# Fewer bytes in the SBUF copies, five of sixteen issued by GpSimd, tau on GpSimd's queue, and a new table of priorities

## The chip, the cores and the metric

The kernel runs on one core of a Trainium2 chip. The time is device microseconds of one execution; the figure that counts is the median of several runs of the same program. An engine is TensorE (PE, with PEld for its weight loads), VectorE (DVE), ScalarE (ACT), GpSimd (POOL) or SyncE (SP, which here only issues DMAs).

## What is computed

Attention over 4 batches x 8 heads, 576 positions, head width 64, with a threshold below the row's maximum; then two feed-forward layers over 2304 tokens, model width 512, inner width 2048, all in float32:

```python
scores = scale * np.matmul(q, k.transpose(0, 1, 3, 2))
thresh = np.max(scores, axis=-1, keepdims=True) - tau
scores = np.where(scores >= thresh, scores, -1000000000.0)
attn = np.exp(scores - np.max(scores, axis=-1, keepdims=True))
attn = attn / (np.sum(attn, axis=-1, keepdims=True) + 1e-09)
attn_out = np.matmul(attn, v)                                   # heads are put side by side: x, 2304 x 512
h = x @ w_in;   x = np.where(h > 0.0, h, np.exp(np.minimum(h, 0.0)) - 1.0) @ w_out
h = x @ w2_in;  x = np.maximum(0.01 * h, h) @ w2_out
```

## The kernel before

**Stages.** Attention is cut into 32 groups: a pair of heads (16 of them) times a half of the query rows, in units of 64 rows; a group has 4 or 5 units. Beside attention, TensorE runs the first half (inner slices f = 0 to 7) of the first feed-forward layer over seven blocks of 256 tokens, as the attention output of those tokens comes free. When attention ends its memory is closed, and the rest follows: one block of 512 tokens with f = 0 to 7, then all tokens in blocks of 512 with f = 8 to 15, then the second layer with f = 0 to 15.

**A unit.** `qk` (L458) writes the scores of a unit to PSUM tile `s`, out of the loaded tile `in`. VectorE scales them and finds the row's maximum (L462, into `ss`) and makes the threshold (`thr`, L468). ScalarE applies the threshold (L473) and the exponential (L476, into `e`). VectorE takes the reciprocal of the sum (`su`, L479), GpSimd multiplies `e` by it (L481).

**Turning.** The matmul with v (L564) needs `e` with keys on the partitions. In the first four groups TensorE transposes it (L496). In the other 28, VectorE transposes 32x32 blocks into a tile `t` (L501), and sixteen DMAs inside SBUF, 32 partitions each, bring the blocks of `t` into their places in a tile `p` (L550): copy (a, d) goes from quadrant a of `t` to quadrant d of `p`. Each row of such a copy holds five column blocks c = 0 to 4. A score row has 576 keys, which is 4.5 times 128, so of the fifth block the partitions 64 to 127 (quadrants d = 2 and 3) are zeros. Of the sixteen copies SyncE issues 13 and GpSimd 3. The matmul runs `v` a group later (`held`).

**Feed-forward beside and after it.** `step_h` (L603 in full float32 for the first block, L606 in three passes for the others) fills PSUM tile `h`; ScalarE takes its exponential (L621), VectorE or GpSimd subtract one (L623, L625), VectorE merges with `h` (L629, into `g`, in the first block into `gh`), ScalarE rounds the result to `gh` (L311), and VectorE or GpSimd form the rest `gl` = g - gh (L305, L306). `step_y` (L656, L660) multiplies by the second weights two steps later.

**Weights** come as raw 64-bit words (`wraw`, L324) and are put together by GpSimd or ScalarE (L328, L336) and by VectorE in two steps (L341, L344); then `split_w` rounds them (`wih`, `woh`, L309 or L311) and takes the rest (`wil`, `wol`). For f = 8 to 15 and for the second layer all weights pass one after the other through a single buffer `w15`.

**Order.** Nothing is scheduled on the chip: `Order.run` lists every engine's instructions when the program is built. Each operation has a due time (`vt`) that is worked out from the table `KN`, and the operations that are ready are taken in that order with assumed costs; letters in `KN` say which engines may do an operation (`ko`: the rest of a weight outside the first eight slices; `kv`: the copy of the v matmul's result out of PSUM). On the chip each engine takes its list in order and waits where an operand isn't there.

Of the kernel before, what the change touches and what calls it, by code (L numbers as in the profile page):

```python
# [259 lines left out]
def attn_moe_kernel(ctx, tc, kqv, tau, w1i, w1o, w2i, w2o, yp, out):  # L260
# [21 lines left out]
    ysx = mp.tile([128, KC, TB], F32, name="ysx")  # L282
    ys_r = Ring(lambda: ysx, 1)
# [133 lines left out]
    ld = op(sp(128, 4, lambda: nc.sync.dma_start(out=taut, in_=tau.partition_broadcast(128))), [], [], KN["tl"])  # L417
    tau_op = op((DVE, 450, taus), [ld], [], -9e5)
# [3 lines left out]
    def group(gi, p, vts):  # L422
# [4 lines left out]
        kq, v = in_r.new(), v_r.new()  # L427
        cut = 2 * HALF + 128 * n
        ld = [op(sp(128, 4 * cut, lambda: nc.sync.dma_start(
            out=kq()[:, 0:cut], in_=kqv[gi * NE + p][:, 0:cut])), [], [kq], due)]  # L430
        lv = op(sp(128, 2560, lambda: nc.sync.dma_start(
            out=v().rearrange("p h c d -> p (h c d)"), in_=kqv[gi * NE + p][:, KQV - 10 * D:KQV])), [], [v], due + KN["vl"])

# [104 lines left out]
        return lambda: values(gi, p, n, w, vts[n - 1] + KN["o3"], by_pe, turned, tg, pg, v, lv, blocks)  # L538

    def values(gi, p, n, w, vt, by_pe, turned, tg, pg, v, lv, blocks):  # L540
        b, u0, u1 = GROUPS[gi]
        got = turned
        if not by_pe:
            got = []
            for z, (a, d) in enumerate((a, (a + r) % 4) for r in range(4) for a in range(4)):
                to = pg, slice(32 * d, 32 * d + 32), slice(5 * a * w, 5 * a * w + 5 * w)
                fr = tg, slice(32 * a, 32 * a + 32), slice(5 * d * w, 5 * d * w + 5 * w)
# [192 lines left out]
    for gi, (b, u0, u1) in enumerate(GROUPS):  # L740
        for p in range(NE):
            later = group(gi, p, [(u + j) * TU for j in range(u1 - u0)])
            u += u1 - u0
            if held is not None:
                held()
            held = later
            if gi < GP or p in PT or u == NP * NU:
                held()
                held = None
        ends.append((b * S + 64 * u1, u))  # L750
# [116 lines left out]
```

## Time and profile before

| | |
|---|---|
| median of 3 runs | 1052.46 us (1051.07 to 1056.69) |
| the profiled execution, its own time | 1050.85 us |
| its span, first to last instruction | 1049.1 us |
| busy PE / DVE / ACT / POOL | 1007.5 / 599.6 / 497.4 / 307.4 us |
| mean granted TensorE clock | 0.992 |

The profiled execution is 1.6 us below the median of the runs and lies within their range; 1.75 us of its time are outside the span. Attention ends at about 408 us of the span. Busy times overlap, so they don't add up to the span; the idle time of TensorE is what a change can win.

### The profile page before, as it was taken

What the parts mean: (1) busy time and instruction counts of PE and PEld (TensorE: products, weight loads), DVE (VectorE), ACT (ScalarE), POOL (GpSimd) and SP (SyncE); (2) the same over time, 40 slices, a digit from 0 to 9 for tenths busy, and PEclk for the clock granted to TensorE, in tenths of its full rate; (3) what the DMA queues carried; (4) which work ended last, traced back from release to release, by engine and by line L of the source; (5) the groups of instructions that cost most, each with busy time, mean ns of one, the idle gap of its engine ahead of it and who ended that gap; (6) DMA issues with size and microseconds to landing.
All of it is one profiled execution on the core that took longest, in us unless ns stands there. A gap on an engine that the chain in (4) does not pass through costs nothing.

```text
span 1049.1 us, 17092 instructions
## 1 busy us (share of the span) xinstructions
PE 1007.5 (96%) x6228; PEld 794.7 (76%) x6228; DVE 599.6 (57%) x1194; ACT 497.4 (47%) x991; POOL 307.4 (29%) x441
## 2 busy tenths in 40 slices
PE   6869989999999999999999999999999999999998
PEld 3446666767667777888888889888888888888898
DVE  6888788788887875888887448642211311211221
ACT  5968667686767763555454234532222212322221
POOL 4678856565655660222232002210000000000000
PEclk8989999999999999999999999999999999999999
DMA  6676877788777765353534103410100100000010
GB/s 209 211 219 172 219 212 210 209 223 224 200 203 217 217 167 151 121 181 101 160 102 139 41 1 105 129 48 1 41 1 1 41 1 1 10 31 1 0 42 21
DMA packets 48564, 120.14 MB, mean 115 GB/s; under 512 B 9888, under 2 KB 14496, under 8 KB 48480
## 3 DMA queue, kind: packets, MB, share of 16 engines
q1 hardware_dynamic: 45792, 111.18, 36.0%
q0 software_dynamic: 2688, 7.87, 2.8%
q8 instruction: 49, 0.80, 0.3%
q14 instruction: 35, 0.29, 0.1%
HBM read 67.63 MB, written 9.44 MB: 73 GB/s over the span
## 4 chain that ended last, share of the span: by engine, by line
PE 81%; DMA 5%; DVE 5%; ACT 4%; issue 2%; SPq 2%; POOL 1%; DVEq 0%; ACTq 0%; POOLq 0%
PE y L660 35%; PE h L606 20%; PE hb L606 15%; PE v L564 5%; PE s L458 4%; DMA p<-t 3%; SPq L550 2%; DMA in<-in_kqv_dram 2%; PE y L656 1%; ACT e L476 1%; DVE t L501 1%; DVE ss L462 1%; ACT ss L473 1%; PE h L603 1%; DVE thr L468 1%
## 5 line engine op out<-in xcount | busy, mean ns | idle before, releaser
L660 PE MATMUL y<-gh,woh 128*128 128x512 f32 (+1 forms) x704 | 245.8, 349 | 2.8 <-ACT ysx L316 2.0
L305 DVE TENSOR_TENSOR gl<-g,gh 128x512 fp32r<-128x512 f32 (+1 forms) x143 | 91.6, 641 | 271.4 <-ACT g L638 257.7
L660 PE MATMUL y<-gl,woh 128*128 128x512 f32 (+1 forms) x704 | 242.7, 345 | 0.0
L606 PE MATMUL h<-xh,wih 128*128 128x256 f32 (+1 forms) x448 | 153.2, 342 | 9.3 <-DVE g L629 4.6
L660 PEld LDWEIGHTS y<-gh,woh 128*128 128x128 f32 x704 | 132.6, 188 | 30.9 <-issue 10.1
L606 PE MATMUL h<-xl,wih 128*128 128x256 f32 (+1 forms) x448 | 148.4, 331 | 0.3 <-DVE xl L305 0.3
L660 PEld LDWEIGHTS y<-gl,woh 128*128 128x128 f32 x704 | 132.7, 188 | 16.1
L481 POOL TENSOR_SCALAR e<-e,su 128x576 f32<-128x576 f32 x144 | 114.5, 805 | 39.9 <-DVE su L479 35.1
L660 PE MATMUL y<-gh,w 128*128 128x256 f32 (+1 forms) x384 | 124.9, 325 | 0.0
L473 ACT ACTIVATE ss<-ss,thr 128x576 f32<-128x576 f32 x144 | 104.4, 767 | 34.1 <-DVE thr L468 33.3
L660 PE MATMUL y<-gh,wol 128*128 128x512 f32 (+1 forms) x320 | 117.7, 368 | 0.0
L462 DVE TENSOR_SCALAR_CACHE_REDUCE ss<-s,scl 128x576 f32<-128x576 f32 x144 | 113.3, 797 | 3.7 <-PE s L458 3.4
L476 ACT ACTIVATE e<-ss,taun 128x577 f32<-128x577 f32 x144 | 110.3, 767 | 0.6
L606 PEld LDWEIGHTS h<-xh,wih 128*128 128x128 f32 x448 | 84.2, 188 | 33.1 <-issue 8.3
L501 DVE STREAM_TRANSPOSE t<-e 128x640 f32<-128x640 f32 x128 | 102.0, 824 | 11.4 <-POOL e L481 5.6
L458 PE MATMUL s<-in 64*64 64x288 f32 x1152 | 92.3, 430 | 9.9 <-DVE ss L462 7.6
L606 PE MATMUL hb<-xl,wih 128*128 128x512 f32 (+1 forms) x256 | 94.5, 369 | 0.0
L606 PE MATMUL hb<-xh,wih 128*128 128x512 f32 (+1 forms) x256 | 94.5, 369 | 0.0
L564 PE MATMUL v<-p,v 128*64 128x320 f32 (+1 forms) x640 | 87.0, 411 | 6.5 <-DMA p<-t 3.3
L606 PEld LDWEIGHTS h<-xl,wih 128*128 128x128 f32 x448 | 84.5, 189 | 9.0 <-DVE xl L305 0.8
L606 PE MATMUL h<-xh,w 128*128 128x256 f32 (+1 forms) x288 | 89.2, 310 | 0.0
L636 ACT ACTIVATE gh<-h 128x512 fp32r<-128x512 f32 (+1 forms) x40 | 22.2, 555 | 137.5 <-PE h L606 137.5
(204 smaller groups left out, 1539.7 us busy)
## 6 DMA issues: line engine op xcount, KB each, us to landing
p<-t SPq DMA_DIRECT2D x208, 100.0 KB, 2.9
p<-t SPq DMA_DIRECT2D x156, 80.0 KB, 3.2
v<-in_kqv_dram SPq DMA_DIRECT2D x32, 320.0 KB, 4.1
in<-in_kqv_dram SPq DMA_DIRECT2D x16, 608.0 KB, 4.4
in<-in_kqv_dram SPq DMA_DIRECT2D x16, 544.0 KB, 3.9
wraw<-in_w1i_dram SPq DMA_DIRECT2D x16, 512.0 KB, 4.2
wraw<-in_w1o_dram SPq DMA_DIRECT2D x16, 512.0 KB, 3.6
wraw<-in_w2i_dram SPq DMA_DIRECT2D x16, 512.0 KB, 3.5
```

What stands on the lines that cost most here:

```text
L305: return pick(who, D=(dve(n), lambda: nc.vector.tensor_tensor(**args()), PORT), P=(pool_tt(n), lambda: nc.gpsimd.tensor_tensor(**args())))
L458: nc.tensor.matmul(s[z]()[64 * h:64 * h + 64, i, 0:HALF], q()[r, at:at + 64], k()[r, h], start=True, stop=True)
L462: om = [op((DVE, dve(S) + 160, lambda z=z: nc.vector.tensor_scalar(out=ss[z]()[:, 0:S].rearrange("p (j c) -> p j c", j=2), in0=s[z]()[:, : ...
L473: o = op((ACT, act(S) + 95, lambda z=z: nc.scalar.activation(out=ss[z]()[:, 0:S], in_=ss[z]()[:, 0:S], func=AF.Prelu, bias=thr()[:, z:z + ...
L476: oe.append(op((ACT, act(S) + 190, lambda z=z: nc.scalar.activation(out=e[z]()[:, 0:S + 1], in_=ss[z]()[:, 0:S + 1], func=AF.Exp, bias=tau ...
L481: on = [op(pick(KN["kn"], P=(pool_ts(S) + 90, lambda z=z: nc.gpsimd.tensor_scalar(out=e[z]()[:, 0:S], in0=e[z]()[:, 0:S], scalar1=su()[:, ...
L501: turned.append(op((DVE, dve(SX) + 70, lambda z=z, cols=cols: nc.vector.transpose(out=blocks(tg).rearrange("p d c q -> p c d q")[:, :, :, ...
L550: q.dma_start(out=to[0]()[to[1], to[2]], in_=fr[0]()[fr[1], fr[2]])
L564: nc.tensor.matmul(ps()[64 * h:64 * h + 64, 0:64 * n], v()[:, h, c, :], blocks(pg)[:, 2 * h:2 * h + 2, c], start=(c == 0), stop=(c == 4))
L606: nc.tensor.matmul(hp(), w_()[:, cs], x_()[:, 0:tb], start=(k == 0 and z == 0), stop=(k == KC - 1 and z == 2))
L636: o1 = op((ACT, actp(tb), lambda: nc.scalar.activation(out=gh()[:, cs], in_=hp(), func=AF.Prelu, alpha=0.01)), [o], [hg, gh], vt)
L660: nc.tensor.matmul(ysl(yg, m), w_()[:, cs], g_()[:, 0:tb], start=(first and z == 0 and share == 0), stop=(last and z == 2 and end))
```

## The change

Four edits, and a new table.

1. The tiles `p` are two fixed tiles. Where the width of a group differs from the one that the tile held last, GpSimd clears block c = 4 of its partitions 64 to 127 (`memset`, 14 of them in all), and the copies into quadrants 2 and 3 leave that block out: 4 instead of 5 column blocks.
2. `NG` = 5: of the sixteen copies of a group GpSimd issues five and SyncE eleven. All five are of the short kind.
3. `tau` is fetched by a DMA on GpSimd's queue at the program's start, and no longer by SyncE between its first loads.
4. The result of a block of 256 is put into a tile `ysa` of the attention stage's memory, that of 512 into `ysb` of the memory after it, where one tile served both.
5. `KN` has other numbers. Two letters change: `ko` from D to P (48 subtractions on 128x512 tiles go from VectorE to GpSimd: 16 for f = 8 to 15 of the first layer, 32 for the second layer) and `kv` from D to AD (10 of 32 copies of v's result go from VectorE to ScalarE).

`PM` is empty, so what the diff makes depend on it does nothing here.

```diff
-NG = 3
+NG = 5
 POOLI = 520
-SPI = 690
+SPI = 720
+PM = ()
+SKIP = True
...
-    pad=18, stay=1957.74, late=1.3, margin=0, look=0.00348273, warm=2, tu=1933.47, lead=15925.1, wv0=975.379,
+    pad=18, stay=1957.74, late=1.3, margin=0, look=0.00236881, warm=2, tu=2525.65, lead=19496.6, wv0=975.379,
...
+    ysx.append(ac.tile([128, KC, TA], F32, name="ysa"))
+    taut = ac.tile([128, 1], F32, name="taut")
+    nc.gpsimd.dma_start(out=taut, in_=tau.partition_broadcast(128))
...
-    p_r = ring(ap_, 2, [128, 20 * WT], F32, "p")
+    pts = [ac.tile([128, 20 * WT], F32, name=f"p{j}") for j in range(2)]
+    p_r = Ring(itertools.cycle(pts).__next__, 2)
+    widths = [None, None]
...
-    ld = op(sp(128, 4, lambda: nc.sync.dma_start(out=taut, in_=tau.partition_broadcast(128))), [], [], KN["tl"])
-    tau_op = op((DVE, 450, taus), [ld], [], -9e5)
+    tau_op = op((DVE, 450, taus), [], [], -9e5)
...
+        if SKIP and not by_pe and widths[which] != w:
+            turned.append(op((POOL, 600, lambda: nc.gpsimd.memset(blocks(pg)[64:128, :, 4], 0.0)), [], [pg], vts[0]))
+        widths[which] = w
...
-                to = pg, slice(32 * d, 32 * d + 32), slice(5 * a * w, 5 * a * w + 5 * w)
-                fr = tg, slice(32 * a, 32 * a + 32), slice(5 * d * w, 5 * d * w + 5 * w)
+                m = 4 * w if SKIP and d > 1 else 5 * w
+                to = pg, slice(32 * d, 32 * d + 32), slice(5 * a * w, 5 * a * w + m)
+                fr = tg, slice(32 * a, 32 * a + 32), slice(5 * d * w, 5 * d * w + m)
...
-                    got.append(op(sp(32, 20 * w, lambda copy=copy: copy(nc.sync), SPI), turned, [pg, tg],
+                    got.append(op(sp(32, 4 * m, lambda copy=copy: copy(nc.sync), SPI), turned, [pg, tg],
```

Three places show how the lists move. VectorE, where the first groups that go through `t` begin (about 62 us of the trace), before:

```order
L344 SCALAR_TENSOR_TENSOR w_705<-wraw,w_705 128x512
L462 TENSOR_SCALAR ss_106,nm<-s,scl 128x576
L341 SCALAR_TENSOR_TENSOR w_742<-wa__746,w_742 128x512
L468 TENSOR_SCALAR thr<-nm,taup 128x2
L344 SCALAR_TENSOR_TENSOR w_742<-wraw,w_742 128x512
```

and from the next scores on:

```order
L462 TENSOR_SCALAR ss_107,nm<-s,scl 128x576
L629 SCALAR_TENSOR_TENSOR gh<-g,h 128x256
L501 STREAM_TRANSPOSE t_88<-e_90 128x5x4x32
L501 STREAM_TRANSPOSE t_88<-e_91 128x5x4x32
L468 TENSOR_SCALAR thr<-nm,taup 128x1
L479 RECIPROCAL su<-su 128x2
L629 SCALAR_TENSOR_TENSOR gh<-g,h 128x256
```

and now (each line number is some 16 to 18 higher: L479 is L462 of before, L518 is L501, L647 is L629):

```order
L346 SCALAR_TENSOR_TENSOR w_700<-wraw,w_700 128x512
L518 STREAM_TRANSPOSE t_88<-e_90 128x5x4x32
L479 TENSOR_SCALAR ss_106,nm<-s,scl 128x576
L343 SCALAR_TENSOR_TENSOR w_737<-wa__741,w_737 128x512
L485 TENSOR_SCALAR thr<-nm,taup 128x2
L346 SCALAR_TENSOR_TENSOR w_737<-wraw,w_737 128x512
L496 RECIPROCAL su<-su 128x2
L479 TENSOR_SCALAR ss_107,nm<-s,scl 128x576
L647 SCALAR_TENSOR_TENSOR gh<-g,h 128x256
L485 TENSOR_SCALAR thr<-nm,taup 128x1
L647 SCALAR_TENSOR_TENSOR gh<-g,h 128x256
```

The second step of a weight has moved from between the transposition and the scores of `ss_106` to ahead of the transposition, and the second `gh` stands ahead of two transpositions instead of behind them.

SyncE, the copies of a group of five units and then of one of four, before (the `in` and `v` rows are loads for later groups):

```order
L550 DMA p<-t_88 32x800 x13
L429 DMA in<-in_kqv_dram 128x1088
L431 DMA v<-in_kqv_dram 128x640
L550 DMA p<-t_87 32x640 x13
L429 DMA in<-in_kqv_dram 128x1088
```

and a group of four now:

```order
L438 DMA v<-in_kqv_dram 128x640
L436 DMA in<-in_kqv_dram 128x1088
L568 DMA p_86<-t_88 32x640 x2
L568 DMA p_86<-t_88 32x512
L568 DMA p_86<-t_88 32x640
L568 DMA p_86<-t_88 32x512
L568 DMA p_86<-t_88 32x640
L568 DMA p_86<-t_88 32x512
L568 DMA p_86<-t_88 32x640 x4
L438 DMA v<-in_kqv_dram 128x640
```

Eleven copies stand between two sets of loads instead of thirteen, three of them shorter by a fifth.

VectorE, the weights of the last slices f = 14 and 15 ahead of the second half of the first layer, before (`w_5648` and `w_5685` are one buffer in turn; `wol` and `wil` are the rests):

```order
L341 SCALAR_TENSOR_TENSOR w_5648<-wa__5655,w_5648 128x512
L344 SCALAR_TENSOR_TENSOR w_5648<-wraw,w_5648 128x512
L305 TENSOR_TENSOR wol_5675<-w_5648,woh_5668 128x512
L623 TENSOR_SCALAR g<-g 128x512
L629 SCALAR_TENSOR_TENSOR g<-g,hb 128x512
L341 SCALAR_TENSOR_TENSOR w_5685<-wa__5687,w_5685 128x512
L305 TENSOR_TENSOR gl<-g,gh 128x512
L344 SCALAR_TENSOR_TENSOR w_5685<-wraw,w_5685 128x512
L305 TENSOR_TENSOR wil_5719<-w_5685,wih_5712 128x512
L623 TENSOR_SCALAR g<-g 128x512
L629 SCALAR_TENSOR_TENSOR g<-g,h 128x512
L341 SCALAR_TENSOR_TENSOR w_5726<-wa__5728,w_5726 128x512
```

and GpSimd there now, where the list of before has rows of L328 alone for these weights (L330 is L328 of before):

```order
L308 TENSOR_TENSOR wil_5642<-w_5616,wih_5635 128x512
L330 TENSOR_SCALAR wa__5655<-wraw 128x512
L308 TENSOR_TENSOR wol_5681<-w_5653,woh_5676 128x512
L330 TENSOR_SCALAR wa__5696<-wraw 128x512
L308 TENSOR_TENSOR wil_5722<-w_5692,wih_5717 128x512
L330 TENSOR_SCALAR wa__5732<-wraw 128x512
L308 TENSOR_TENSOR wol_5766<-w_5730,woh_5757 128x512
L330 TENSOR_SCALAR wa__5794<-wraw 128x512
L308 TENSOR_TENSOR w_5823<-w_5782,wih_5817 128x512
```

The subtraction has left VectorE's list and alternates with the first step of the next weight on GpSimd.

## Rows read from the trace of the kernel before

**Rows 1.** Busy time by stage: us; PE, PEld, DVE, ACT, POOL; clock; DMA; GB/s.

```profile
0.00:57.00 57.00, 43.44 (x354) 23.18 (x354) 44.35 (x106) 45.57 (x86) 33.38 (x51) 0.91 0.65 212
57.00:76.00 19.00, 12.91 (x72) 8.16 (x72) 15.22 (x35) 12.77 (x25) 13.65 (x19) 0.82 0.76 222
76.00:408.00 332.00, 314.70 (x2728) 225.81 (x2730) 261.92 (x611) 222.09 (x491) 202.00 (x306) 1.00 0.74 203
408.00:1049.10 641.10, 636.44 (x3077) 537.54 (x3073) 278.11 (x444) 216.93 (x390) 58.37 (x67) 1.00 0.18 57
```

**Rows 2.** TensorE's waits, 76 to 408 us: total us, times, longest.

```profile
PE h L606 <- DVE g L629: 4.6, 9, 0.7
PE h L606 <- ACT g L621: 3.8, 7, 0.7
PE v L564 <- DMA p<-t: 3.3, 3, 1.6
PE s L458 <- DMA in<-in_kqv_dram: 2.3, 2, 1.9
PE y L660 <- ACT ysx L316: 2.0, 3, 0.7
```

**Rows 3.** Timeline of TensorE, 60 to 78 us: start, us, what, idle before.

```profile
64.33 0.72 PE L458 MATMUL s<-in 64*64 64x288 f32 x8 [2.20 <-DVE ss L462]
66.46 1.24 PE L458 MATMUL s<-in 64*64 64x288 f32 x8 [1.42 <-DVE ss L462]
69.10 3.53 PE L603 MATMUL h<-x,w 128*128 128x256 f32 x8 [1.40 <-DVE gh L629]
72.47 1.89 PE L656 MATMUL y<-gh,w 128*128 128x256 f32 x8
...
76.75 1.53 PE L564 MATMUL v<-p,v 128*64 128x320 f32 x8 [1.09 <-DMA p<-t]
```

**Rows 4.** Timeline of VectorE, 61 to 70 us.

```profile
62.89 0.65 DVE L344 SCALAR_TENSOR_TENSOR w<-wraw,w 128x512 uint32<-128x512 uint32 x1
...
66.66 1.56 DVE L501 STREAM_TRANSPOSE t<-e 128x640 f32<-128x640 f32 x2
...
68.64 0.40 DVE L629 SCALAR_TENSOR_TENSOR gh<-g,h 128x256 f32<-128x256 f32 x1
```

**Rows 5.** Timeline of SyncE's queue, first 13 us.

```profile
1.19 0.42 SPq L417 DMA_DIRECT2D taut<-in_tau_dram  x1
```

**Rows 6.** The copies' line: ns least, median, most; first and last start.

```profile
L550 SPq DMA_DIRECT2D p<-t x364: 507/590/1869, 63.0 to 399.7; - x182
...
L550 POOL DMA_DIRECT2D p<-t x84: 496/498/689, 64.0 to 393.0; - x84
```

**Rows 7.** SyncE's waits, 100 to 350 us: total us, times, longest.

```profile
SPq L550 <- DVE t L501: 10.7, 6, 3.5
SPq L550 <- DMA in<-in_kqv_dram: 2.9, 3, 2.1
```

**Rows 8.** GpSimd, 100 to 350 us in ten stretches: sum, and mean of 25 us.

```profile
sum 250.00, POOL 152.43; mean POOL 15.24
```

**Rows 9.** Clearing a 128x64 tile on GpSimd: ns.

```profile
L386 POOL MEMSET e<- x4: 151/151/151, 0.7 to 1.0; 128x64 f32 x4
```

**Rows 10.** Clearing a 128x128 tile on GpSimd: ns.

```profile
masks.py:197 POOL MEMSET ident<- x1: 204/204/204, 1.1 to 1.1; 128x128 f32 x1
```

**Rows 11.** GpSimd's groups by form: count, busy us, mean ns, idle before.

```profile
L306 POOL TENSOR_TENSOR w<-w,wih 128x512 fp32r<-128x512 f32 x8 | 10.2, 1279 | 1.4 <-PE y L656 1.3
```

**Rows 12.** The rests of slices 8 to 15, 410 to 495 us: VectorE's row.

```profile
L305 DVE TENSOR_TENSOR wil<-w,wih x8: 679/692/1124, 415.5 to 483.4; 128x512 fp32r<-128x512 f32 x8
```

**Rows 13.** Timeline, 415 to 416.2 us: the first of these rests.

```profile
415.46 0.68 DVE L305 TENSOR_TENSOR wil<-w,wih 128x512 fp32r<-128x512 f32 x1
```

**Rows 14.** Timeline, 482 to 487.2 us: the last of them and its first use.

```profile
483.40 0.69 DVE L305 TENSOR_TENSOR wil<-w,wih 128x512 fp32r<-128x512 f32 x1 [0.70 <-ACT wih L311]
...
486.90 0.39 PE L606 MATMUL hb<-xh,wil 128*128 128x512 f32 x1
```

More of the change, by code (lines that the diff above doesn't have):

```diff
@@ L33 @@
 WT = 32 * UM
-KQV = 2 * HALF + 128 * UM + 10 * D
 BESIDE = 7
@@ L37 @@
 PT = ()
-NG = 3
+NG = 5
 POOLI = 520
-SPI = 690
+SPI = 720
+PM = ()
+SKIP = True
+QW = 2 * S if PM else 128 * UM
+KQV = 2 * HALF + QW + 10 * D
 NATIVE = 1
@@ L281, in attn_moe_kernel @@
     wa_r = ring(stg, 1, [128, 512], F32, "wa_")
-    ysx = mp.tile([128, KC, TB], F32, name="ysx")
-    ys_r = Ring(lambda: ysx, 1)
+    ysx = []
+    ys_r = Ring(lambda: ysx[-1], 1)
     wdst = {}
@@ L415, in taus, with group @@
                                 op0=ALU.is_ge, op1=ALU.mult)
[L417 to L418 removed]
+    tau_op = op((DVE, 450, taus), [], [], -9e5)
     xready = {}
[L422 removed]
+    def group(gi, p, vts, held=None):
         b, u0, u1 = GROUPS[gi]
@@ L426, in group @@
         due = vts[0] - KN["lead"]
[L427 to L432, printed above, removed]
+        at0 = 2 * HALF
+        if held is None:
+            kq, v = in_r.new(), v_r.new()
+            cut = 2 * HALF + (2 * S if b in PM else 128 * n)
+            ld = [op(sp(128, 4 * cut, lambda: nc.sync.dma_start(
+                out=kq()[:, 0:cut], in_=kqv[gi * NE + p][:, 0:cut])), [], [kq], due)]
+            lv = op(sp(128, 2560, lambda: nc.sync.dma_start(
+                out=v().rearrange("p h c d -> p (h c d)"), in_=kqv[gi * NE + p][:, KQV - 10 * D:KQV])), [], [v],
+                due + KN["vl"])
+        else:
+            kq, v, ld, lv = held
+            at0 += 128 * u0
+        mine = kq, v, ld, lv
         def k():
@@ L437, in q @@
         def q():
-            return kq()[:, 2 * HALF:cut]
+            return kq()[:, at0:at0 + 128 * n]
         by_pe = gi < GP or p in PT
+        which = len(p_r.gens) % 2
         pg, tg = p_r.new(), None if by_pe else t_r.new()
@@ L739, in attn_moe_kernel @@
     TU, u, ends, held = KN["tu"], 0, [], None
[L740 to L750, printed above, removed]
+    order = []
+    for b in range(B):
+        mine = [gi for gi, g in enumerate(GROUPS) if g[0] == b]
+        order += [(gi, p) for p in range(NE) for gi in mine] if b in PM else [(gi, p) for gi in mine for p in range(NE)]
+    kept, ready = None, {}
+    for gi, p in order:
+        b, u0, u1 = GROUPS[gi]
+        kept, later = group(gi, p, [(u + j) * TU for j in range(u1 - u0)], kept if b in PM and u0 else None)
+        u += u1 - u0
+        ready[b * S + 64 * u1] = u
+        if held is not None:
+            held()
+        held = later
+        if gi < GP or p in PT or u == NP * NU:
+            held()
+            held = None
+    ends = sorted(ready.items())
     TE = u * TU
@@ L757, in close_attn @@
         late_pool.append(sbuf(ctx, "mb"))
+        ysx.append(late_pool[0].tile([128, KC, TB], F32, name="ysb"))
         late["psb"] = ctx.enter_context(tc.tile_pool(name="psb", bufs=1, space=PSUM))
```

19 lines of the change are left out of this document (9 added, 10 removed).

## The prediction, made before the changed kernel ran

> **What bounds the kernel now.** I read the stages first. From 408 us to the end TensorE is busy 636.4 of 641.1 us at full clock [rows 1]; the matmuls are the same before and after, so that stage can only be spoiled. From 76 to 408 us TensorE is busy 314.7 of 332 us and idle 17.3; from 57 to 76 us it is busy 12.9 of 19 us, at a granted clock of 0.82; the first 57 us hold 13.6 us of idle time, most of it the chain of the first units, where nothing else is there to run. So the most that can be won after the start is 6.1 + 17.3 us of idle time and what the low clock cost, about 2.5 % of the whole. The reader should see that neither 57 % VectorE nor the DMA share decides: it is which operand TensorE finds missing.
>
> Next the waits of TensorE in 76 to 408 us [rows 2]: 8.4 us in 16 waits before `h`, until VectorE or ScalarE have taken the earlier `h` out of its bank; 3.3 us before the v matmul for copies `p<-t`; 2.3 us before scores for the load `in`; 2.0 us and another 0.8 for the evacuation of `y`. In 57 to 76 us the timeline shows four holes of 2.20, 1.42, 1.40 and 1.09 us, and one run of eight matmuls that took 3.53 us where the next run of eight of the same shape took 1.89 [rows 3]: after the holes the clock had gone from its upper level (2.4 GHz) to the lower (1.2 GHz).
>
> Last, the queue that serves the copies. SyncE's median copy takes 590 ns to issue [rows 6], a group has 13 of them and two loads besides, and a group lasts about 11.6 us (332 us over 28.5 groups). SyncE's first two waits in 250 us sum to 13.6 us [rows 7]; all nine that the view lists, to 25.7. It is thus issuing or walking its list nine tenths of the time, and a load `in` that stands behind thirteen copies comes when they are out, not when it is needed.
>
> **The change, part by part.**
>
> *Start.* The load of tau took 0.42 us of SyncE's queue, ahead of the first weight [rows 5]; the weights' first conversion ends the wait from which the chain goes on. Everything behind moves up by it: -0.4 us. On GpSimd's queue tau may land later than it did. It is needed with the first scores, and VectorE has slack until the first weight is there, so I count nothing for it; bounds -0.4 and +1.
>
> *57 to 76 us.* VectorE's lists [rows 4] put the hole at 64.33 behind a weight's second step of 0.65 us, which now stands earlier: -0.6. The hole at 69.10 ended with the second `gh`, which stood behind two transpositions of 1.56 us together; now it stands ahead of them. TensorE's scores before it end at 67.7, so 1.4 of it go: -2.0 in all. With smaller holes the clock may stay up: the slow runs cost 3.53 - 1.89 and 1.24 - 0.72, that is 2.2 us [rows 3]. The holes become smaller but don't vanish; I take half, -1.0, with bounds 0 and -2.2.
>
> *SyncE.* Two copies less for each group are 2 x 0.59 = 1.2 us of 11.6, and three of the eleven carry a fifth less. SyncE's share falls from about nine tenths to eight, and the loads that stand behind the copies are issued 1.2 us earlier each group. That covers the longest wait for `in`, 1.9 us, in good part, and the waits for copies. Of 3.3 + 2.3 = 5.6 us I take 4.0 as gone; bounds 0 and -5.6.
>
> The Trainium skill (DMA: Bandwidth & Descriptors, section Issuing engines are not separate DMA queues) speaks against this: a second issuing engine saves only the time on the sequencer, which it calls usually small. Here 13 issues of 590 ns are two thirds of a group [rows 6], so the trace doesn't bear out "small"; by the rule this term would be near 0.
>
> *Waits before `h`.* In TensorE's list of before, 11 of the steps `h` in attention follow the previous `h` directly, with nothing between to cover the exponential; now 8 do. At 8.4 / 16 = 0.53 us a wait [rows 2] three fewer are -1.6. The rest of the new order may open others; I take -1.5, bounds -4 and +2.
>
> *GpSimd.* It issues two copies more for each of 28 groups, 2 x 0.498 us [rows 6], in all 28 us, and clears 14 times 512 or 640 elements. A clearing of 64 elements took 0.15 us and of 128 0.20 [rows 9, 10]; the step between them is 0.8 ns an element, so 640 are some 0.6 us, and 14 at most 9 us; by the lower row alone 2 us. GpSimd is busy 15.2 of 25 us [rows 8], so about 130 us of 332 are free and 37 find room. What hides them is that idle time; if it weren't there, they would stand ahead of the multiplication of `e` and come back as the third rival below. I take 0.
>
> *Weights after attention.* The subtraction for slices 8 to 15 took VectorE 0.69 us [rows 12]; on GpSimd the same form took 1.28 [rows 11]. All sixteen weights share one buffer, so this is a chain. The first rest ended at 416.14 [rows 13], the fifteenth at 484.09, and its first matmul began at 486.90 [rows 14]: a period of 67.95 / 14 = 4.85 us, a margin of 2.8 us. The new first one ends 0.6 later, so the period may grow to (486.9 - 416.7) / 14 = 5.01 before TensorE waits. The step alone makes it 5.44, but VectorE's queue holds one operation less in each round, and its waits go. Without relief the wait is 14 x 0.43 = 6 us, with full relief nothing. No row says how much of the period is waiting in that queue; I take the middle between 4.85 and 5.44, some 5.1, and 14 x 0.09 = +1.3. This is the only term in the long stage.
>
> The Trainium skill (SBUF — State Buffer, section Who interferes with whom) has VectorE with two SBUF inputs and GpSimd lock each other out for a whole instruction. The row agrees that something does: the subtraction's median of 0.69 us rises to 1.12 at most [rows 12]. By the rule the relief on VectorE would shrink and the term go towards 6 us.
>
> The ten copies of v's result on ScalarE and the two result tiles cost the same work on engines that TensorE didn't wait for at those places: 0. Sum: -0.4 - 2.0 - 1.0 - 4.0 - 1.5 + 1.3 = -7.6 us. Against the profiled execution that is 1050.85 - 7.6 = 1043.3; that execution lay 1.6 us below the median of 1052.46, so for a median I take 1052.46 - 7.6 = 1044.9, say **1045 us**.
>
> **The rivals.**
>
> *The relief is hidden.* The waits for DMAs vanish, but another wait ends last at the same places: most of TensorE's waits already name VectorE or ScalarE [rows 2], and the new order gives them as much. Left are start and the 57 us stretch with its clock, -3.4, and +1.3: 1050.4 us. Against it: loads and copies end waits alone, up to 1.9 us at once.
>
> *Weights too late.* All gains of the forecast, but no relief in the chain: +6 in place of +1.3, 1049.6 us. It decides from a period of 5.01 us on.
>
> *GpSimd late.* The other side. GpSimd takes its list in order; five issues in a row, and a clearing that must wait until the matmul with `v` has read the tile, stand ahead of the multiplication of `e`, and VectorE's transpositions and so the copies wait. Price: of 37 us a third reaches TensorE, 12.3, and the gain for copies and `h` is lost: 1052.46 - 3.4 + 1.3 + 12.3 = 1062.7; a fifth gives 1057.8. From 7.6 us of the 37 on, with the other gains kept, the change loses. For it: GpSimd's waits would be new and no row shows them; against it: 40 % of its time is free.
>
> **How the numbers follow.** Chances: forecast 0.54, hidden 0.23, weights 0.09, GpSimd late 0.14. The forecast's own range goes from all bounds of gain together (-0.4 - 2.0 - 2.2 - 5.6 - 4.0 = -14.2, 1038.3) to 1049. The range to hold 8 in 10 goes from 1038 to 1056: below is almost nothing, above is most of the last rival. Half a per cent, 5.3 us, is about what a measurement of this kernel can tell from no change. Faster than 1047.2 is most of the forecast (0.46) and a piece of the next two (0.05): 0.51. Slower than 1057.7 is GpSimd late and a little more: 0.14. The rest, 0.35, is no change.
>
> **What would show it.** In the new profile: from 57 to 76 us the hole before the second `h` run gone and the clock above 0.9; SyncE's waits in 100 to 350 us well above 25.7 us, because it has time; TensorE's waits for `p<-t` and `in` under 2 us; GpSimd busy 17 to 18 of 25 us in the attention stage, with no wait of VectorE's transposition on it of more than before; the rest of the fifteenth weight 0 to 3 us after its matmul could start, and no other idle time after 408 us. The forecast is wrong if TensorE's idle time in 76 to 408 us doesn't fall below 14 us, or if the clearing or the copies of GpSimd show up as what ended its idle time.

## The result, and the profile after

The changed kernel takes 1043.74 us (median of 4 runs, 1042.33 to 1044.41), the kernel before in the same session 1053.38 (4 runs): ratio 0.9893, interval 0.9867 to 0.9920. That is faster, by 9.6 us of medians; the two profiled executions differ by only 6.4 (1050.85 and 1044.41; spans 1049.1 and 1042.6), since the one of before lies below all four of its runs (the lowest took 1051.07, so it does not lie within their range, as the section on the time before has it), and that of the changed kernel is the slowest of its four. In a later session one of 17 runs of the kernel before took 1440.6 us at a mean granted clock of 0.65; it is left out below. The account is made in spans: 6.5 us. Lines of the changed kernel are numbered higher (in some of the experiments by a few more): `qk` L475, scores' scaling L479, turning L518, copies L568, `v` L582, `h` L621 and L624, `y` L674 and L678, clearing L461.

Busy time by stage of the changed kernel, in the columns of [rows 1]:

```profile
0.00:57.00 57.00, 43.21 (x354) 23.48 (x354) 43.58 (x106) 45.85 (x87) 35.41 (x53) 0.91 0.65 212
57.00:76.00 19.00, 12.28 (x70) 7.40 (x70) 16.65 (x35) 13.47 (x27) 14.25 (x21) 0.91 0.76 220
76.00:408.00 332.00, 319.18 (x2754) 231.06 (x2755) 252.33 (x615) 232.29 (x511) 230.62 (x365) 0.99 0.70 195
408.00:1042.60 634.60, 630.52 (x3051) 533.33 (x3050) 256.66 (x391) 215.36 (x387) 111.68 (x106) 1.00 0.17 55
```

TensorE's idle time from 76 to 408 us has fallen from 17.3 to 12.8 us, though this stretch now takes in the turn to the stage after attention. Its waits there, against [rows 2]:

```profile
PE h L624 <- ACT g L639: 5.1, 10, 0.5
PE h L624 <- ACT xh L313: 2.5, 1, 2.5
PE v L582 <- DMA p<-t: 2.2, 1, 2.2
PE h L624 <- DVE g L647: 1.7, 3, 0.6
PE y L678 <- ACT ysa L318: 1.4, 2, 0.7
```

No wait for `in` is left and one for `p<-t`, the first `v` behind copies. The waits before `h` are 13 of 6.8 us instead of 16 of 8.4. New is one of 2.5 us for `xh`. Around 57 to 76 us, where [rows 3] had four holes:

```profile
64.79 0.72 PE L475 MATMUL s<-in 64*64 64x288 f32 x8 [2.41 <-DVE ss L479]
66.92 1.24 PE L475 MATMUL s<-in 64*64 64x288 f32 x8 [1.42 <-DVE ss L479]
68.09 3.06 PE L621 MATMUL h<-x,w 128*128 128x256 f32 x8
70.99 1.89 PE L674 MATMUL y<-gh,w 128*128 128x256 f32 x8
...
76.56 2.02 PE L582 MATMUL v<-p,v 128*64 128x320 f32 x7 [2.20 <-DMA p<-t]
```

The hole before the second `h` run is gone, but the first is longer (2.41 for 2.20), the run of eight `h` still takes 3.06 us for 1.89, so the clock fell all the same, and the hole before `v` is 2.20 instead of 1.09. At 76.6 us the kernel is only 0.2 us ahead. SyncE's waits from 100 to 350 us, against [rows 7], and GpSimd's sum and mean of the same stretch, against [rows 8]:

```profile
SPq L568 <- DVE t L518: 30.6, 13, 5.7
SPq L438 <- PE v L582: 9.9, 2, 5.3
SPq L568 <- DMA in<-in_kqv_dram: 5.7, 4, 2.2
SPq L436 <- PE s L475: 5.0, 4, 1.7
```

```profile
sum 250.00, PE 243.49 PEld 176.26 DVE 198.04 ACT 184.13 POOL 182.12; mean PE 24.35 PEld 17.63 DVE 19.80 ACT 18.41 POOL 18.21
```

SyncE's first four waits alone are 51 us; its whole list sums to 61.4 us where that of before sums to 28.2 (the prediction's 25.7 are only the nine longest of fourteen rows). GpSimd is busy 18.2 of 25 us for 15.2. Its new work, by form:

```profile
L568 POOL DMA_DIRECT2D p<-t x140 | 70.5, 508 | 23.1 <-DVE t L518 9.5 <-PE s L475 5.4 <-DVE ss L479 3.0
L461 POOL MEMSET p<- 64x640 f32 x8 | 5.0, 627 | 1.6 <-POOL e L498 0.7 <-issue 0.5
L461 POOL MEMSET p<- 64x512 f32 x6 | 3.1, 519 | 0.7 <-issue 0.4
```

So 56 more issues at 0.508 us are 28.4 us and the clearings 8.1 us, as the prediction sized them.

**Account of the 6.5 us.** From the start to the `v` at 76.6 us: 0.2 won. From there to the first `h` of the stage after attention 325.5 us for 332.5: 7.0 won. From that `h` to the end 640.5 us for 639.8: 0.7 lost. Inside the 7.0, TensorE's losses from one matmul's start to the next, above 0.45 us each: for `in` and for copies 5.8 us in 5 places before (one of them a `v` of 0.55 us for which no releaser is seen) and none now; before `h` (for `g` and `gh`) 12.2 in 17 places before and 9.0 in 13 now; at the turn of the stages 1.0 before and 2.75 now. The turn of before, whose counterpart stands with n3 below:

```profile
409.29 0.50 PE L606 MATMUL h<-xh,wih 128*128 128x512 f32 x1 [0.72 <-ACT xh L311]
```

### The profile page after: what moved, and what is told of

It reads as the page before. It is cut to its first block, busy times and chain, and to the rows that moved or that the text cites. A ratio compares the mean times of both kernels' runs of the same rounds, so it can differ in the third digit from the quotient of the medians.

```text
span 1042.6 us, 17014 instructions
## 1 busy us (share of the span) xinstructions
PE 1005.2 (96%) x6228; PEld 795.3 (76%) x6228; DVE 569.2 (55%) x1146; ACT 507.0 (49%) x1009; POOL 392.0 (38%) x542
## 4 chain that ended last, share of the span: by engine, by line
PE 90%; DVE 3%; DMA 2%; ACT 2%; issue 1%; POOL 0%; SPq 0%; ACTq 0%; DVEq 0%; POOLq 0%
PE y L678 37%; PE h L624 22%; PE hb L624 15%; PE v L582 7%; PE s L475 7%; PE y L674 1%; DMA p<-t 1%; PE h L621 1%; DVE w L346 1%; DMA taut<-in_tau_dram 1%; DVE ss L479 1%; DMA wraw<-in_w1i_dram 1%; PE y L513 0%; DVE xl L307 0%; ACT e L493 0%
## 5 line engine op out<-in xcount | busy, mean ns | idle before, releaser
L307 DVE TENSOR_TENSOR gl<-g,gh 128x512 fp32r<-128x512 f32 (+1 forms) x150 | 101.1, 675 | 284.4 <-ACT g L656 265.0
L678 PE MATMUL y<-gh,woh 128*128 128x512 f32 (+1 forms) x704 | 245.5, 349 | 2.1 <-ACT ysa L318 1.4
L678 PE MATMUL y<-gl,woh 128*128 128x512 f32 (+1 forms) x704 | 242.8, 345 | 0.0
L624 PE MATMUL h<-xh,wih 128*128 128x256 f32 (+1 forms) x448 | 153.1, 342 | 9.2 <-ACT g L639 5.1
L678 PEld LDWEIGHTS y<-gh,woh 128*128 128x128 f32 x704 | 132.5, 188 | 29.1 <-issue 8.8
L624 PE MATMUL h<-xl,wih 128*128 128x256 f32 (+1 forms) x448 | 148.6, 332 | 0.7 <-DVE xl L307 0.6
L678 PEld LDWEIGHTS y<-gl,woh 128*128 128x128 f32 x704 | 132.7, 188 | 16.1
L678 PE MATMUL y<-gh,w 128*128 128x256 f32 (+1 forms) x384 | 124.9, 325 | 0.0
L479 DVE TENSOR_SCALAR_CACHE_REDUCE ss<-s,scl 128x576 f32<-128x576 f32 x144 | 113.8, 798 | 10.9 <-PE s L475 10.7
L678 PE MATMUL y<-gh,wol 128*128 128x512 f32 (+1 forms) x320 | 117.7, 368 | 0.0
L518 DVE STREAM_TRANSPOSE t<-e 128x640 f32<-128x640 f32 x128 | 101.2, 823 | 17.9 <-POOL e L498 12.5
L624 PEld LDWEIGHTS h<-xh,wih 128*128 128x128 f32 x448 | 84.2, 188 | 33.2 <-issue 8.8
L475 PE MATMUL s<-in 64*64 64x288 f32 x1152 | 91.3, 428 | 7.8 <-DVE ss L479 7.8
L624 PE MATMUL hb<-xh,wih 128*128 128x512 f32 (+1 forms) x256 | 94.6, 369 | 0.0
L624 PE MATMUL hb<-xl,wih 128*128 128x512 f32 (+1 forms) x256 | 94.5, 369 | 0.0
L582 PE MATMUL v<-p,v 128*64 128x320 f32 (+1 forms) x640 | 87.1, 417 | 5.3 <-DVE p L319 2.3
L624 PEld LDWEIGHTS h<-xl,wih 128*128 128x128 f32 x448 | 84.3, 188 | 10.0 <-DVE xl L307 1.8
L624 PE MATMUL h<-xh,w 128*128 128x256 f32 (+1 forms) x288 | 89.3, 310 | 0.0
```

The source lines that it names most:

```text
L307: return pick(who, D=(dve(n), lambda: nc.vector.tensor_tensor(**args()), PORT), P=(pool_tt(n), lambda: nc.gpsimd.tensor_tensor(**args())))
L475: nc.tensor.matmul(s[z]()[64 * h:64 * h + 64, i, 0:HALF], q()[r, at:at + 64], k()[r, h], start=True, stop=True)
L479: om = [op((DVE, dve(S) + 160, lambda z=z: nc.vector.tensor_scalar(out=ss[z]()[:, 0:S].rearrange("p (j c) -> p j c", j=2), in0=s[z]()[:, : ...
L518: turned.append(op((DVE, dve(SX) + 70, lambda z=z, cols=cols: nc.vector.transpose(out=blocks(tg).rearrange("p d c q -> p c d q")[:, :, :, ...
L582: nc.tensor.matmul(ps()[64 * h:64 * h + 64, 0:64 * n], v()[:, h, c, :], blocks(pg)[:, 2 * h:2 * h + 2, c], start=(c == 0), stop=(c == 4))
L624: nc.tensor.matmul(hp(), w_()[:, cs], x_()[:, 0:tb], start=(k == 0 and z == 0), stop=(k == KC - 1 and z == 2))
```

## The experiments

Theory A is the prediction's: SyncE's queue, relieved by five copies on GpSimd and fewer bytes, gave most of the gain. Theory B: the new table's order gave it, the copies were hidden. Where a run keeps the lists of a kernel, every engine's instructions stand in that kernel's order, and only what the diff shows is different (a copy that changes its issuer stands in the other queue at the place where the program gives it out). The kernel before ran beside each of three batches, with medians of 1053.7 (n1 to n4), 1053.9 (n5 to n8) and 1054.0 us (n9 to n12).

**n1: the new lists, fewer copies on GpSimd, full length.**

```diff
-                    got.append(op((POOL, POOLI, lambda copy=copy: copy(nc.gpsimd)), turned, [pg, tg], vt + KN["o4"],
+                    got.append(op((POOL, POOLI, lambda copy=copy, z=z: copy(
+                        nc.gpsimd if z * 3 // 16 != (z + 1) * 3 // 16 else nc.sync)), turned, [pg, tg], vt + KN["o4"],
...
-                to = pg, slice(32 * d, 32 * d + 32), slice(5 * a * w, 5 * a * w + m)
-                fr = tg, slice(32 * a, 32 * a + 32), slice(5 * d * w, 5 * d * w + m)
+                to = pg, slice(32 * d, 32 * d + 32), slice(5 * a * w, 5 * a * w + 5 * w)
+                fr = tg, slice(32 * a, 32 * a + 32), slice(5 * d * w, 5 * d * w + 5 * w)
...
-            turned.append(op((POOL, 600, lambda: nc.gpsimd.memset(blocks(pg)[64:128, :, 4], 0.0)), [], [pg], vts[0]))
+            turned.append(op((POOL, 600, lambda: pg()), [], [pg], vts[0]))
```

> Every list of TensorE, ScalarE and VectorE is that of the changed kernel, but the copies are those of before: all sixteen of full length, three of them issued by GpSimd, thirteen by SyncE, and nothing is cleared. Theory A (SyncE's queue, the prediction's largest term): the waits for `in` and `p<-t` come back, TensorE's idle time in 76 to 408 us goes from 12.8 to some 17 us, SyncE's waits in 100 to 350 us fall from some 59 to under 30 us, and the time is 1048 to 1051 us. Theory B (the new order does it, the copies are hidden): 1043 to 1045 us, no wait for `in`, waits for `p<-t` under 3 us.

The edit was not what the expectation says: of the five places that are GpSimd's only one fits the rule for three, so GpSimd issued one copy of sixteen and SyncE fifteen. Measured: 1081.46 us, ratio 1.0260 (1.0228 to 1.0293). This lies outside the ranges of both theories, but neither was about fifteen copies on SyncE; with them the new order is far slower than the kernel before. n5 below is the run that was meant.

```profile
PE v L583 <- DMA p<-t: 15.5, 10, 5.2
PE v L583 <- issue: 6.1, 8, 1.7
```

`v` waits 15.5 us for copies, and 6.1 more where no releaser is seen.

**n5, n6, n7: issuer and bytes apart, new lists.** n5 and n6 choose the issuer as below, n5 and n7 have the full length and no clearing by the other lines of n1, and n7 leaves five copies on GpSimd.

```diff
-                def copy(q, to=to, fr=fr):
+                def copy(q, to=to, fr=fr, z=z):
+                    ng = 3
+                    q = nc.gpsimd if z * ng // 16 != (z + 1) * ng // 16 else nc.sync
                     q.dma_start(out=to[0]()[to[1], to[2]], in_=fr[0]()[fr[1], fr[2]])
```

> The order of the changed kernel on TensorE, ScalarE and VectorE, and the copies of before as they really were: 16 of full length, 3 issued by GpSimd and 13 by SyncE, no clearing. (In n1 the edit had left GpSimd one copy of sixteen and SyncE fifteen.) Theory A (SyncE's queue is the limit and the new order has less slack for it): between n1 and the changed kernel, 1050 to 1062 us, with waits of the v matmul for `p<-t` of 4 us or more in 76 to 408 us. Theory B (the old copies suffice for the new order, n1 was only beyond the edge): 1043 to 1046 us, waits for `p<-t` under 3 us.

> The changed kernel in all but the issuer: three of sixteen copies by GpSimd and thirteen by SyncE, short where they are short now, with the clearing. If the issuer carries the gain of the copies, as the prediction has it, the time is that of n5 less at most 2 us; if the bytes carry it, it is that of the changed kernel, 1043 to 1045 us.

> The changed kernel in all but the bytes: all sixteen copies of full length, no clearing, five issued by GpSimd. If the issuer carries the gain, 1043 to 1046 us, with SyncE's waits in 100 to 350 us some 5 to 15 us below the 59 of the changed kernel; if the bytes carry it, the time of n5.

Measured: n5 1063.18 us, ratio 1.0084 (1.0062 to 1.0105); n6 1063.72, 1.0079 (1.0048 to 1.0110); n7 1047.98, 0.9945 (0.9925 to 0.9964). n5 lies 1.2 us above the range of theory A, and n7 some 2 us above the range put for the issuer. In these lists, which were made for five copies on GpSimd, the issuer carries most of it: with three on GpSimd the shorter copies change nothing that can be seen, with five on GpSimd they are worth some 4 us by the medians. n7's runs are spread wide (1045.44 to 1052.21) and the profiled one is the fastest of them, so its trace doesn't show where these 4 us go. n5 and n6 lose their 20 us in attention: from the first `v` behind copies to the turn they take 345.1 and 344.8 us, the changed kernel 325.5. In n5 some 8 us of this are waits for copies and loads and at most 3.4 the clock behind them; the rest is made of smaller pieces and is not accounted for in full.

What a late copy costs in n5, in TensorE's timeline and in stretches of 6 us (columns of [rows 1]):

```profile
141.79 0.28 PE L680 MATMUL y<-gh,w 128*128 128x256 f32 x1
144.29 0.61 PE L584 MATMUL v<-p,v 128*64 128x256 f32 x2 [2.23 <-DMA p<-t]
145.49 1.12 PE L584 MATMUL v<-p,v 128*64 128x256 f32 x4 [0.58 <-DMA v<-in_kqv_dram]
```

```profile
134.00:140.00 6.00, 5.47 (x53) 4.11 (x55) 5.25 (x11) 2.35 (x8) 4.77 (x8) 1.00 0.75 213
140.00:146.00 6.00, 3.19 (x31) 1.90 (x25) 2.94 (x9) 5.95 (x13) 5.13 (x8) 0.90 0.76 202
146.00:152.00 6.00, 6.00 (x48) 4.04 (x45) 2.51 (x5) 0.29 (x3) 0.33 (x1) 0.81 0.68 179
```

After holes of 2.2 and 0.6 us the granted clock is 0.90 and 0.81, so part of these stretches runs at 1.2 instead of 2.4 GHz: such a hole can be paid for twice. Over 76 to 420 us the low clock costs n5 at most 5.1 us, the changed kernel 1.7 and the kernel before nothing (one minus the granted clock, summed over stretches of 4 us; where TensorE stands idle at the low clock it costs nothing).

The Trainium skill (DMA: Bandwidth & Descriptors, section Issuing engines are not separate DMA queues) says that a second issuing engine saves only sequencer time, usually small. What is saved here is indeed only that, two issues of 0.59 us in a group. With lists made for five copies it is not small: n6, which differs from the changed kernel in the issuer alone, is 20 us slower. How much of this is the queue and how much the lists that no longer fit, n9 below asks.

**n8: eight copies on GpSimd, new lists.** The edit of n6 with `ng = 8`.

> The changed kernel with eight of sixteen copies issued by GpSimd, all else in the same order: 84 issues of 0.51 us more on GpSimd, 43 us. By the rival of the late GpSimd its multiplications of `e` come late: from 18.2 of 25 us GpSimd goes to 21 to 22, and the time to 1050 us or more. If its free time still covers them, 1042 to 1044.5 us, and SyncE's waits in 100 to 350 us rise above 80 us.

Measured: 1063.98 us, ratio 1.0087 (1.0064 to 1.0110). The rival of the late GpSimd is real three copies further on, in lists that were made for five; lists made for eight were not run.

```profile
PE v L584 <- DMA p<-t: 9.1, 9, 2.9
PE h L626 <- ACT g L641: 5.2, 11, 0.5
PE h L626 <- DVE g L649: 1.9, 4, 0.6
PE h L626 <- POOL xl L308: 1.8, 1, 1.8
```

```profile
sum 250.00, PE 235.78 PEld 173.72 DVE 193.38 ACT 171.46 POOL 200.76; mean PE 23.58 PEld 17.37 DVE 19.34 ACT 17.15 POOL 20.08
```

GpSimd is busy 20.1 of 25 us, not full; but it takes its list in order, `v` waits nine times for copies, and one `h` waits 1.8 us for a rest of x that GpSimd forms late. At the waits of 0.7 us and more the copy that lands last is one of GpSimd's; it takes 4.4 to 6.4 us from issue to landing, against a median of 3.3 for all of GpSimd's copies in this run. SyncE and GpSimd at one of them, and the `v` that waits:

```profile
333.97 0.53 SPq L436 DMA_DIRECT2D in<-in_kqv_dram  x1
334.60 0.58 SPq L733 DMA_DIRECT2D yp_dram<-ysa  x1
334.90 1.03 POOL L570 DMA_DIRECT2D p<-t  x2
341.87 1.51 PE L584 MATMUL v<-p,v 128*64 128x256 f32 x10 [1.73 <-DMA p<-t]
```

SyncE, with eight copies instead of eleven, is through with its own and has issued the next load and a store of 512 KB. GpSimd's last two copies come behind them and land after 5.9 and 6.4 us; SyncE's last two copies, issued ahead of the load, took 2.5 and 2.7.

**n2: the old lists with the new copies.** The copies of the changed kernel in the kernel before; block 4 is cleared ahead of the group's first copy.

```diff
-                to = pg, slice(32 * d, 32 * d + 32), slice(5 * a * w, 5 * a * w + 5 * w)
+                m = 4 * w if d > 1 else 5 * w
+                to = pg, slice(32 * d, 32 * d + 32), slice(5 * a * w, 5 * a * w + m)
...
-                def copy(q, to=to, fr=fr):
+                def copy(q, to=to, fr=fr, z=z):
+                    if clear[0]:
+                        nc.gpsimd.memset(blocks(pg)[64:128, :, 4], 0.0)
+                        clear[0] = False
+                    if z * 5 // 16 != (z + 1) * 5 // 16:
+                        q = nc.gpsimd
+                    elif q is nc.gpsimd:
+                        q = nc.sync
```

> Every list of TensorE, ScalarE and VectorE is that of the kernel before, and so are tau, the result tile and the table; only the copies are the new ones: a fifth less in quadrants 2 and 3, five of sixteen issued by GpSimd, block 4 cleared once where the width changes, just ahead of the first copy of the group. Theory A: 4 us of the 5.6 us of waits for `in` and `p<-t` go, 1047 to 1050 us. Theory B: the waits stay, or others take their place: 1052 to 1054 us. If the clearing stands in the way, because it must wait for the matmul with v here, slower than 1054.

Measured: 1050.11 us, ratio 0.9963 (0.9945 to 0.9981), just above the range of theory A and below that of theory B. The copies alone are worth 3.6 us of medians, close to the prediction's 4.0, but not most of the 9.6. Of TensorE's waits for a DMA over 76 to 408 us one line is left:

```profile
PE v L578 <- DMA p<-t: 0.4, 1, 0.4
```

**n9, n10: lists written anew.** n9 is the changed kernel with another `NG`, n10 with the whole table and `SPI` of before.

```diff
-NG = 5
+NG = 3
```

```diff
-SPI = 720
+SPI = 690
...
-    pad=18, stay=1957.74, late=1.3, margin=0, look=0.00236881, warm=2, tu=2525.65, lead=19496.6, wv0=975.379,
+    pad=18, stay=1957.74, late=1.3, margin=0, look=0.00348273, warm=2, tu=1933.47, lead=15925.1, wv0=975.379,
...
```

> The changed kernel with NG = 3, short copies where they are short now, and the lists written anew for it (in n6 the lists were those made for five). Theory S (the loss of n5 and n6 is SyncE's queue, too full for this table of priorities): 1055 us or more again. Theory O (the loss of n6 is that lists made for one set of copies were run with another): 1043 to 1051 us, with waits for `p<-t` under 3 us.

> The changed kernel with the numbers and letters of the table of before (and SPI = 690), lists written anew: so the copies, tau and the result tiles without the new table. If the table carries the gain that n2 lacks (n2 1050.1, the changed kernel 1043.7), the time is 1048 to 1053 us; if it was only that n2's lists were made for other copies, 1043 to 1046 us.

Measured: n9 1057.85 us, ratio 1.0033 (1.0017 to 1.0048); n10 1058.57, 1.0038 (1.0023 to 1.0052). Neither fewer copies on GpSimd with the new table nor the new copies with the old table gains anything, although the lists are made for them; both also carry the new result tiles, whose price follows below. n9 fits neither theory as it was put: waits for `p<-t` are down to 1.3 us, as theory O has it, but the time is not, since 21 waits before `h` now cost 11.9 us. n10 lies above both ranges put for it. Its last run of `v` in attention starts at 395.9 us, no later than the 396.5 of the changed kernel; but TensorE then still has feed-forward work to do until 409.5 us, which the changed kernel has behind it by then. Some 8.7 us are thus lost ahead of the turn; what is seen of them are 19 waits of 9.3 us before `h`, against 13 of 6.8. Another 2.9 are lost at the turn (below). From the first `v` behind copies to the turn n10 takes 337.1 us, 4.5 more than the kernel before, and the turn alone accounts for 4.6 of that: without the new result tiles n10 might be no slower than before in this stretch, which was not run.

**n3, n4, n11: what the change cost after attention.** n3 has one result tile in memory of its own, n4 the letter `ko` = D, n11 both. The edit of n3:

```diff
+    mp = sbuf(ctx, "moe")
...
-    ysx = []
-    ys_r = Ring(lambda: ysx[-1], 1)
+    ysx = mp.tile([128, KC, TB], F32, name="ysx")
+    ys_r = Ring(lambda: ysx, 1)
...
-    ysx.append(ac.tile([128, KC, TA], F32, name="ysa"))
...
-        ysx.append(late_pool[0].tile([128, KC, TB], F32, name="ysb"))
```

and n4's edit, in the table:

```diff
-    ... ko='P', ...
+    ... ko='D', ...
```

> The changed kernel with one result tile for all blocks, in memory that lives through the whole program, as before; all lists are in the same order. If the first tiles of the memory after attention wait because `ysa` lies in the memory that is closed, until its last store is through, then TensorE's loss at the turn of the stages falls from 2.75 us at 402 us to some 1.0, and the time by 1.7 us, to 1042.0. If the loss there has another cause (the activation of `xh` comes late by itself), it stays at 2.7 us and the time at 1043.7.

> The changed kernel with the rests of the weights outside the first eight slices on VectorE again (ko = D); the lists of attention are the same. If the rests on GpSimd cost what the new profile shows (0.6 us at 643.6 us where the rest of x waits behind one of them), the time falls by 0.5 to 0.7 us, to 1043.1; if VectorE has no room for them, TensorE's idle time after 408 us grows above 6.4 us, and the time with it. By the prediction's term of +1.3 us for the chain of weights it would fall to 1042.4.

> The changed kernel with one result tile for the whole program (n3) and the rests outside the first eight slices on VectorE (n4). By the profiles of n3 and n4 TensorE's loss at the turn of the stages falls from 2.75 to 1.0 us and the 0.6 us at 644 us is gone: 2.3 us less than the changed kernel, 1041.4 us. If the starts of the executions differ by as much as n3's did, 1042 to 1043.5 us.

Measured: n3 1042.82 us, ratio 0.9892 (0.9864 to 0.9920); n4 1044.49, 0.9914 (0.9888 to 0.9941); n11 1041.37, 0.9885 (0.9869 to 0.9901). By the intervals none differs from the changed kernel, so that what follows rests on the traces and not on the times. ScalarE and TensorE at the turn, changed kernel:

```profile
401.39 2.20 ACT L313 ACTIVATE xh<-x 128x512 fp32r<-128x512 f32 x4 [9.63 <-DMA yp_dram<-ysa]
```

```profile
402.07 0.50 PE L624 MATMUL h<-xh,wih 128*128 128x512 f32 x1 [2.46 <-ACT xh L313]
```

and n3:

```profile
402.62 1.67 ACT L314 ACTIVATE xh<-x 128x512 fp32r<-128x512 f32 x3 [7.86 <-PE v L582]
```

```profile
403.31 0.50 PE L624 MATMUL h<-xh,wih 128*128 128x512 f32 x1 [0.72 <-ACT xh L314]
```

With `ysa` in the memory that is closed, the first tile of the memory after it waits until `ysa`'s last store has landed; with one tile elsewhere it waits for the `v` matmul alone, and TensorE's loss from start to start is 1.0 instead of 2.75 us (n3 and n11 alike). In n10 the store comes last of all, and the loss at the turn is 5.6 us:

```profile
414.54 2.20 ACT L313 ACTIVATE xh<-x 128x512 fp32r<-128x512 f32 x4 [8.32 <-DMA yp_dram<-ysa]
```

```profile
415.22 0.80 PE L624 MATMUL h<-xh,wih 128*128 128x512 f32 x1 [5.47 <-ACT xh L313]
```

The other loss is at 644 us; GpSimd, VectorE and TensorE of the changed kernel:

```profile
642.19 1.64 POOL L308 TENSOR_TENSOR wil<-w,wih 128x512 fp32r<-128x512 f32 x1 [3.79 <-ACT wih L313]
```

```profile
641.39 2.98 DVE L307 TENSOR_TENSOR xl<-x,xh 128x512 fp32r<-128x512 f32 x3
```

```profile
644.43 0.50 PE L624 MATMUL h<-xl,wih 128*128 128x512 f32 x1 [0.41 <-DVE xl L307]
```

Three subtractions that take 0.69 us each alone take 2.98 while GpSimd forms the rest of a weight, and TensorE loses 0.6 us. n4 and n11 show no such loss. The profiled execution of n4 is no faster all the same: after its hole of 2.74 us at the turn, where `ysa` was left as it was, eight `h` matmuls start 0.42 us apart, at 1.2 GHz; in the changed kernel's profiled execution the matmuls after the same hole stayed at 0.23, but for a few.

**n12: the first copied group.** n11, with eight copies on GpSimd in that group alone (the edit of n6 with `ng = 8 if (gi, p) == (1, 0) else 5`).

> n11, and in the first group that is turned by copies GpSimd issues eight of sixteen, in all later ones five. If SyncE's queue sets the wait of 2.2 us before the v matmul at 76.6 us (there SyncE issues weights between the copies), the wait falls below 1 us and the time by 1 to 2 us against n11; if the landing of the copies sets it, the wait stays, and the multiplications of `e` behind the three more issues may cost up to 1.5 us.

Measured: 1044.64 us, ratio 0.9914 (0.9892 to 0.9935): no gain, and the wait stays. GpSimd's last two of these copies, and the `v` that waits:

```profile
70.61 1.04 POOL L570 DMA_DIRECT2D p<-t  x2
```

```profile
77.29 1.15 PE L584 MATMUL v<-p,v 128*64 128x320 f32 x5 [2.74 <-DMA p<-t]
```

Both queues are through by 71.7 us, but these copies take 6.2 us from issue to landing (median; SyncE's in the same stretch took 5.8 in the changed kernel and 4.3 in the kernel before), with the DMA engines 9 tenths busy by three weight loads of 512 KB at the same time. Landing sets this hole, not the queue.

## Why the prediction was right, point by point

Forecast and result lie 1.3 us apart, and the profile's -6.5 beside the sum of -7.6; but two terms were wrong and one cost was not seen, and that the sum comes out so near is in part luck. By matmul starts the copies and the waits before `h` gave 3.5 us more than forecast and the long stage lost 0.6 less; the start with the stretch up to 76 us gave 3.2 less, and 1.75 went at the turn. Of the signs, those on TensorE's idle time (12.8 us, under 14) and SyncE's waits came; TensorE's waits for `p<-t`, 2.2 us, stayed above 2, GpSimd's 18.2 of 25 us just above 18.

*Start and 57 to 76 us, with the clock: -3.4 predicted, -0.2 measured.* The step that failed is that "VectorE's lists [rows 4] put the hole at 64.33 behind a weight's second step of 0.65 us, which now stands earlier: -0.6", and behind it the term of the clock, -1.0. That step still stands ahead of the same scaling; what its new place could fill was VectorE's idle time before the transposition in the kernel before:

```profile
62.12 0.84 DVE L501 STREAM_TRANSPOSE t<-e 128x640 f32<-128x640 f32 x1 [0.65 <-POOL e L481]
```

VectorE and GpSimd in the changed kernel:

```profile
61.53 1.73 DVE L346 SCALAR_TENSOR_TENSOR w<-wraw,w 128x512 uint32<-128x512 uint32 x1
61.45 1.26 POOL L308 TENSOR_TENSOR w<-w,woh 128x512 fp32r<-128x512 f32 x1
```

The step, 0.65 us in [rows 4], took 1.73 beside GpSimd's subtraction, and the hole grew to 2.41 us. The Trainium skill (SBUF — State Buffer, section Who interferes with whom) has the two engines share one pair of ports under an exclusive lock; this row and the 2.98 us above agree with it. The hole before the second `h` did go, as predicted, but what it gave went to the next wait in the row: `v` waits 2.20 instead of 1.09 us for the first copies, and n12 shows why an earlier issue doesn't help. The clock of 0.91 looks like a hit and isn't: behind the hole before `v`, after the stretch, the granted clock is 0.64 from 76 to 80 us, and n3, with the same lists, has 0.82 from 57 to 76. The start's -0.4 can't be told: at the last `v` of the fourth group the changed kernel is 0.16 us ahead (56.38 for 56.54), and the executions with its TensorE list lie between 55.8 (n4) and 58.5 us (n1) there.

*SyncE and DMA waits: -4.0 predicted; right.* By the view of waits 5.6 us have become 2.2. From 76.6 us on all 5.8 us are gone by matmul starts; 1.1 came back just ahead, in the first `v`. n2 has the copies alone: -3.6 us of medians.

*Waits before `h`: -1.5 predicted, -1.6 measured* by the view of waits (8.4 to 6.8), 3.2 by matmul starts, with a `gh` among them. There are three waits fewer (16 to 13), as the count of steps that follow one another had it.

*GpSimd: 0 predicted, right for five copies only.* VectorE's transpositions do wait more for it (12.5 us in 16 waits for 5.0 in 8), against the sign that the prediction gave, and this didn't reach TensorE. At eight copies (n8) it is the rival's case: 20 us lost, at 20.1 of 25 us busy.

*Weights after attention: +1.3 predicted, 0 measured.* The chain now, on GpSimd:

```profile
L308 POOL TENSOR_TENSOR wil<-w,wih x8: 1286/1291/1455, 407.2 to 480.9; 128x512 fp32r<-128x512 f32 x8
```

Its period is (480.93 - 407.2) / 14 = 5.27 us, longer than the 5.1 assumed, so the growth was, if anything, put too small. The last rest is done at 482.2, 0.8 us before its first use at 483.06, because TensorE's list changed too, which the term left out:

```profile
474.22 0.39 PE L624 MATMUL h<-xh,wil 128*128 128x512 f32 x1
483.06 0.39 PE L624 MATMUL hb<-xh,wil 128*128 128x512 f32 x1
```

The first uses of the rests stand 5.44 us apart up to the one at 474.22, and the last stands 8.84 behind it, with `y` matmuls between. At 5.44 it would have come at 479.7 and waited some 2.5 us. The cost of moving these subtractions came elsewhere: 0.6 us at 644 us.

*Not foreseen:* the new tile for the result was counted at 0, with the reason that TensorE didn't wait at those places. Its work was the same; its memory was not, and 1.75 us went at the turn.

*What the prediction didn't see at all* is that order and copies belong together. It adds the term for the order to the term for the copies. The runs: copies alone in the old lists -3.6 us, the new lists with the old copies +9.3 (n5), both together -9.6. So the relief of SyncE is shown, by n2 alone and by n5 and n6 in the new lists; the other 6 us need the new table as well, and which of its numbers give them stays open. What makes the new lists so sensitive isn't settled either: n5 shows late copies and the clock behind them, n9 shows that even lists made for three copies lose with this table, by other waits.

## What to carry to other kernels

A list of instructions that is fixed when the program is built fits one set of transfer times: change who issues a few copies and 20 us of TensorE's time can go, since a late operand opens a hole and the clock may fall behind it; lists made anew do not by themselves bring it back (n9). So try such changes together with the order, and don't add their gains. A tile's place in memory is an edge of the schedule as well: whatever still has to be stored out of a memory that is reused stands ahead of the first tile of the next stage. The version with the lowest median keeps the change and takes back its two side effects (n11: 1041.37 us, ratio to the kernel before 0.9885); by its interval it can't be told from the change itself (0.9893).

## What was not expected of the hardware

Issuing a copy costs GpSimd 0.50 us in the median for 64, 80 and 100 KB alike (changed kernel and before); clearing 64 x 640 elements takes 0.63 us, 64 x 512 takes 0.52. With one and the same list on TensorE, VectorE and ScalarE the executions differ early on: TensorE's fifth group of `v` starts at 75.4 us in n7, 76.6 in the changed kernel, and 78.4 in n3. A copy that is issued behind a load and a store takes 5.9 us to land where those ahead of them took 2.5 to 2.7 (n8). And of two holes of 2.7 us at the same place, in the changed kernel and in n4, one was followed by matmuls at the lower clock (n4) and the other was not.
